# Linear attention beside a gated FFN on one core: the query projection of eight token tiles leaves the projection stage and runs as row-tiled pairs ahead of its chunk's gate/up

## The chip, the cores and the metric

The kernel runs on one core of a Trainium2 chip, in one launch, with bf16 inputs and output. The metric is the device time of one execution in microseconds (us). TensorE is called PE below, VectorE DVE, ScalarE ACT, GpSimd POOL, and SyncE, which issues nearly all DMAs, SP.

## The reference, cut to what matters

```python
# S=2048 tokens, D=576, H=32 heads of 18, F=4608
x  = A_x
xn = layernorm(x)                                   # over the 576 columns
q, k, v = split(xn @ wqkv)                          # 576 -> 3*576
phi = lambda t: where(t > 0, t + 1, exp(t)) + 1e-6
pq, pk = phi(q), phi(k)
kv  = einsum("bhsd,bhse->bhde", pk, v)              # per head 18x18
z   = sum over tokens of pk
o   = (pq @ kv) / (pq . z + 1e-6)                   # per head
return x + o @ wo + (gelu(xn @ w_gate) * (xn @ w_up)) @ w_down
```

## The kernel before, in words

The 2048 tokens are 16 tiles of 128 tokens. The kernel has two parts.

**The K stage** takes the tiles one after the other. For tile n, DVE takes the row statistics in two halves (`ln_half`, L224) and joins them (`ln_aggr`, L227), ACT makes 1/std by a Ln and an Exp (`ln_rstd`, L231 and L232), and the tile is normalised into `xn` either by DVE (`ln_norm`, L245) or by ACT (`ln_norm_act`, L240, which needs a small bias that POOL makes, L235); the string `NORM` says which. The normalised tile is transposed into `xnT`, tiles 0 and 1 by PE and a copy, the others by a DMA in the crossbar (`dma_transposes`, L273, on SP's queue). Then PE multiplies K and Q in halves of 288 columns, five matmuls to a half because 576 is four and a half times 128 (`kq_mm`, L281, and `q_first`, L289, for Q of tile 0). Each half has a PSUM bank of its own (K: 4 and 5, Q: 6 and 7), which the next tile uses again. A row of ones at row 64 of the fifth block adds 1 in the matmul, so that phi is max(min(exp(psum-1), 1), psum): ACT makes the exponential (`kq_exp`, L296) and DVE the rest (`kq_phi`, L301), into `pq` and `pk`. V is never formed: PE sums G = xn^T pk over all tiles in banks 0 to 3 (`g_accumulate`, L320, seven matmuls for a tile; a 1 in a column beside pk gives the column sums of xn), and POOL sums pk over the tiles (`z_add`, L210, called z below). `pk` lies in the store that later holds the FFN's hidden values, so its writes are named hT in the profile.

The order in which these steps are recorded is the order of each engine's queue. Each step has a time, a rank and what it must follow; `in_order` makes an order from them. In front of that stands `HEAD`, a list written out by hand, of which this kernel has about half the steps. In the list `s` is a half of the statistics, `a` the join, `r` 1/std, `b` the bias, `n` the normalisation, `c` the transpose, `m6.1.0` the matmuls of tile 6, K (1) or Q (0), half 0, `e` their exponential, `p` their phi, `z` and `G` the sums, `x` a load of two tiles of x. Across engines only semaphores order the work, not the list.

After the last tile come the rest of G (its fourth row block, L320, and a strip of 64 rows, L327), the copies of G, the small product that gives kv (L400) and the sum of z.

**The FFN part** goes over four chunks of 512 tokens. Of each chunk, 18 steps of gate and up (`gu_pair`) put two 128-column blocks each through `_Unit`, then four `_DownTile`s multiply down and add the attention's output. A `_Unit` computes two outputs in two banks. The contraction of 576 is nine blocks of 64 rows; PE is split into two row tiles of 64 that run at the same time, one on each output, and they take turns on a bank: `p1` gives the lower rows to output 0 and the upper to output 1, then an empty instruction on POOL waits for that (`relay`), and `p2` does it the other way round. Parts of neighbouring units alternate: p1 of two units, then p2 of two units. All of this is L351. The down matmuls are L750 and L755, a short row-tiled pair that opens or closes a tile is L738. Banks are handed out by a ring of eight. The denominators of the attention are made by DVE beside gate and up, one tile in four steps (`den_jobs`), 16 jobs in a chunk, tiles 0 to 3 in the first.

```python
SP queue of the FFN part: gate/up blocks (4 buffers ahead), w_down and wo in chunk 0, outputs
ACT: one table of functions holds exp and ln, another gelu; it is loaded where it changes
```

Of the kernel before, what the change touches and what calls it, by code (L numbers as in the profile page):

```python
# [8 lines left out]
ACT = mybir.ActivationFunctionType  # L9
# [31 lines left out]
XW = 640  # L41
KLO = HP + 1
Q_CUT = 3
PKW = 578


class _Ring:
# [11 lines left out]
def kernel(  # L59
# [119 lines left out]
    nc.gpsimd.memset(xn[:, :, D:XW], 0.0)  # L179
    nc.gpsimd.memset(xn[:, :, D:D + 1], 1.0)  # L180
    nc.gpsimd.memset(wqkv_sb[HP:HP + 1, 4, 0:2 * D], 1.0)
    nc.gpsimd.memset(pk[:, :, 0:1], 1.0)
    nc.gpsimd.memset(pk[:, :, D + 1:D + 2], 1.0)

    bmask = const.tile([P, CR], F32, name="bmask")
    g_sb = apool.tile([P, KT, D], BF16, name="g_sb")
# [21 lines left out]

    def z_add(n):
        nc.gpsimd.tensor_tensor(  # L210
            out=z_bf[:] if n == NS - 1 else z_sum[:], in0=pk[:, 0, 1:D + 1] if n == 1 else z_sum[:], in1=pk[:, n, 1:D + 1],
            op=ALU.add,
        )

# [84 lines left out]

    def kq_phi(n, which, hf):  # L300
        nc.vector.scalar_tensor_tensor(  # L301
            out=(pq, pk)[which][:, n, which + hf * HALF:which + (hf + 1) * HALF], in0=e_tiles[n, which, hf][:], scalar=1.0,
            in1=ps_all[:, KQ_BANK[which] + hf, :HALF], op0=ALU.min, op1=ALU.max,
        )

    G_A = {
        0: [(0, 0, 0, 288), (1, 0, 288, 289)],
        2: [(2, 0, 0, 288), (3, 0, 288, 289)],  # L310
        1: [(0, 288, 0, 224), (1, 289, 224, 223), (2, 288, 447, 130)],
    }
    G_B = {3: [(4, 0, 0, 288), (5, 0, 288, 289)]}
    STRIP = ((6, 0, 1, 0), (7, HALF + 1, 0, HALF))
    eps_sum = const.tile([P, KT], F32, name="eps_sum")

    def g_accumulate(n, pieces):
        for kt, ps_ in pieces.items():
            for b, col, d0, w in ps_:
                nc.tensor.matmul(  # L320
                    ps_all[:, b, col:col + w], lhsT=xn[:, n, kt * P:(kt + 1) * P], rhs=pk[:, n, 1 + d0:1 + d0 + w],
                    start=(n == 0 and col == 0), stop=(n == NS - 1), skip_group_check=True,
                )

    def g_strip(n):
        for rows, (b, c0, _, _) in zip((LO, HI), STRIP):
            nc.tensor.matmul(  # L327
                ps_all[rows, b, 0:HALF + 1], lhsT=xn[:, n, 4 * P:D], rhs=pk[:, n, c0:c0 + HALF + 1],
                start=(n == 0), stop=(n == NS - 1), skip_group_check=True,
            )  # L330

# [127 lines left out]
        steps[name] = _Step(*args, **kw)  # L459

    GL = 0.0
    NORM = "DDDAADADADADADAD"
    COPY = ("DVE", "ACT")
    LEAD = (-9.0, 0.5, -0.5, -0.5)
    X_AT = [3.35, 4.40, 6.30, 8.80] + [10.40] * 4
    W_AT = {1: 5.60, 0: (7.65, 8.45)}

    for n0 in range(8, NS, 2):
        step(("x", n0), "SP", 0.50, n0 - 5.5, [], lambda n0=n0: load_x(n0, 2), ready=1.6 * n0 + 2.0, tail=3.0)
    for n in range(NS):  # L470
        lead = LEAD[n] if n < 4 else 0.0
        after_x = [("x", n // 2 * 2)] if n >= 8 else []
# [5 lines left out]
        if n < TD:  # L478
            for i, (k0, k1, eng) in enumerate([(0, 3, "ACT"), (3, KT, COPY[n])]):
                b = TP_BANK[n] - i  # L480
                if NORM[n] == "A":
                    if not i:
                        step(("bias", n), "POOL", 0.20, n - 2.1 + lead, [("rstd", n)], lambda n=n: ln_bias(n))
                    step(("norm", n, i), "ACT", (0.49, 0.36)[i], n - 2.1 + lead, [("bias", n)],
                         lambda n=n, k0=k0, k1=k1: ln_norm_act(n, k0 * P, min(k1 * P, D)))
                else:
                    step(("norm", n, i), "DVE", (0.26, 0.19)[i], n - 2.1 + lead, [("rstd", n)],
                         lambda n=n, k0=k0, k1=k1: ln_norm(n, k0 * P, min(k1 * P, D)), tail=0.05)
                step(("tp", n, i), "PE", (0.32, 0.21)[i] if n == 0 else (0.18, 0.12)[i], n - 1.5 + lead, [("norm", n, i)],
                     lambda n=n, k0=k0, k1=k1, b=b: transposes(n, k0, k1, b), tail=0.08)  # L490
                step(("xnT", n, i), eng, 0.27 if i else 0.44, n - 0.88 + lead, [("tp", n, i)],
                     lambda n=n, k0=k0, k1=k1, b=b, eng=eng: tp_copy(n, k0, k1, b, acopy if eng == "ACT" else vcopy), tail=0.04)
            ready = [("xnT", n, 0), ("xnT", n, 1)]
        else:
            if NORM[n] == "P":
                step(("norm", n), "POOL", 2.35, n - 2.1 - GL, [("rstd", n)], lambda n=n: ln_norm_pool(n))
            elif NORM[n] == "A":
                step(("bias", n), "POOL", 0.15, n - 2.1, [("rstd", n)], lambda n=n: ln_bias(n))
                step(("norm", n), "ACT", 0.77, n - 2.1, [("bias", n)], lambda n=n: ln_norm_act(n), tail=0.09)
            else:  # L500
                step(("norm", n), "DVE", 0.36, n - 2.1, [("rstd", n)], lambda n=n: ln_norm(n), tail=0.07)
            step(("xnT", n), "SP", 2.10, n - 1.9, [("norm", n)], lambda n=n: dma_transposes(n), tail=2.05)
            ready = [("xnT", n)]
        for which, rank in ((1, n), (0, n + 0.6)):
            for h in range(2):
                r = rank + h / 100
                free = [("phi", n - 1, which, h)] if n else []
                if n == which == 0:
                    k0, k1 = ((0, Q_CUT), (Q_CUT, KT))[h]
                    step(("mm", 0, 0, h), "PE", 0.246 * (k1 - k0), r, ready + [("mm", 0, 0, 0)][:h],  # L510
                         lambda k0=k0, k1=k1: q_first(k0, k1), ready=W_AT[0][h], tail=0.15)
                else:
                    step(("mm", n, which, h), "PE", 0.615, r, ready + free, lambda n=n, w=which, h=h: kq_mm(n, w, h),
                         ready=W_AT[which] if which else W_AT[0][1], tail=0.15)
                step(("exp", n, which, h), "ACT", 0.46, r + 0.10, [("mm", n, which, 1 if n == which == 0 else h)],
                     lambda n=n, w=which, h=h: kq_exp(n, w, h), tail=0.03)
                step(("phi", n, which, h), "DVE", 0.37, r + 0.15, [("exp", n, which, h)],
                     lambda n=n, w=which, h=h: kq_phi(n, w, h), tail=0.08)
        if n > 0:
            idle = [("bias" if NORM[n + 4] == "A" else "norm", n + 4)] if n + 4 < NS else []  # L520
            step(("z", n), "POOL", 1.40, n + 2.0, [("phi", m, 1, h) for m in (0, n) for h in range(2)] + idle + ([("z", n - 1)] if n > 1 else []),
                 lambda n=n: z_add(n))
        step(("G", n), "PE", 0.75, n + 1.15, [("phi", n, 1, 0), ("phi", n, 1, 1)], lambda n=n: g_accumulate(n, G_A))
    step(("spin",), "PE", 0.30, -1.0, [("tp", 0, 1)], lambda: spin(5))

    step(("bmask",), "POOL", 0.95, 0.2, [("norm", 2)], make_bmask)
# [2 lines left out]
    def in_order(steps):  # L529
# [15 lines left out]
        return [name for _, _, name in sorted(begun)]  # L545

    HEAD = """
        s0.1 s0.0 a0 r0 s1.1 n0.0 t0.0 n0.1 t0.1 s1.0 a1 w c0.1 s2.0 c0.0 s2.1 m0.1.1 a2 r1 r2 m0.1.0 n1.1 e0.1.1
        t1.1 n1.0 n2 p0.1.1 m0.0.0 t1.0 B s3.0 e0.1.0 s3.1 a3 m0.0.1 c1.1 c1.0 e0.0.0 r3 m1.1.1 p0.1.0 p0.0.0 s4.1
        G0 m1.1.0 e0.0.1 s4.0 b3 c2 g n3 c3 e1.1.1 s5.0 p0.0.1 m1.0.0 e1.1.0 a4 p1.1.1 m1.0.1 s5.1 r4 p1.1.0 e1.0.0  # L550
        a5 m2.1.1 b4 e1.0.1 s6.0 m2.1.0 x8 s6.1 G1 n4 p1.0.0 e2.1.0 p1.0.1 m2.0.0 a6 e2.1.1 s7.0 p2.1.0 r5 m2.0.1
        p2.1.1 n5 z1 m3.1.0 c4 r6 s7.1 e2.0.1 e2.0.0 m3.1.1 G2 c5 p2.0.1 e3.1.0 a7 p2.0.0 p3.1.0 s8.0 b6 e3.1.1
        p3.1.1 z2 m3.0.1 s8.1 n6 a8 e3.0.1 s9.0 m3.0.0 c6 e3.0.0 G3 p3.0.1 s9.1 r7 a9 x10 n7 r8 m4.1.0 e4.1.0 x12
        m4.1.1 e4.1.1 m4.0.1 z3 r9 p3.0.0 m4.0.0 c7 p4.1.0 e4.0.1 p4.1.1 e4.0.0 n9 m5.1.0 p4.0.1 G4 b8 z4 m5.1.1 n8
        e5.1.0 c9
    """
    KIND = {
        "x": "x", "s": "stats", "a": "aggr", "r": "rstd", "b": "bias", "n": "norm", "t": "tp", "c": "xnT", "m": "mm",
# [32 lines left out]
            g_plus_eps(g_sb[rows, 4, i * HALF:(i + 1) * HALF], ps_all[rows, b, c0:c0 + HALF], eps_sum[rows, 4:5], eng)  # L591


    load_w(2)
    nc.sync.dma_start(wqkv_sb[HP:P, 4, 2 * D:], A_wqkv[512:576, 2 * D:])
    for i in range(NWBUF):
        load_gu(i, 0)
        load_gu(i, 1)
    for c0, c1 in ((0, SC), (SC, S)):
        nc.sync.dma_start(xnT[HP:P, 4, c0:c1], xnT[0:HP, 4, c0:c1])  # L600
    for n in range(NS - 2):
        g_accumulate(n, G_B)
    g_accumulate(NS - 1, G_A)
# [42 lines left out]
    def gu_pair(sc, k):  # L646
# [29 lines left out]
        for i, (b, u) in enumerate(units):  # L676
            u.p2()
            gl = fwork.tile([P, SC], F32, name="gl")
            nc.scalar.activation(out=gl[:], in_=ps_all[:, b[0], :], func=ACT.Gelu_apprx_tanh)  # L679
            nc.vector.tensor_tensor(out=hT[:, GUB * k + i, :], in0=ps_all[:, b[1], :], in1=gl[:], op=ALU.mult)  # L680
            if den_jobs and i == 1 and 0 < k < NF // GUB - 1:
                job, n = den_jobs.pop(0)
                job(n)

    def m_product(c, bank):
        rows = DH * HCH[c]
# [81 lines left out]
                nc.sync.dma_start(out_view[:, self.n, :], self.res[:])  # L768

    for sc in range(NSC):  # L770
        for k in range(NF // GUB):
            gu_pair(sc, k)
            if sc == 0 and k in m_last_steps:
                m_last_steps[k]()
        while wd_loaded[0] < NF:
            load_wd_slice()

        tiles = [_DownTile(sc * TPC + j) for j in range(TPC)]
        tiles[0].pair()
        tiles[1].pair()  # L780
# [2 lines left out]
        for j, t in enumerate(tiles):  # L783
# [4 lines left out]
            for hf in range(2):  # L788
                t.down(hf, hooks if j == hf == 0 else {})
                if closed:  # L790
                    t.add(hf)
        for t in tiles[2:]:
            if sc < NSC - 1:
                t.opened = True
# [33 lines left out]
```

## Time and profile before

| what | value |
|---|---|
| five runs | 511.88 to 512.29 us, median 511.94 |
| the profiled execution | its own time 511.9 us, span 510.2 us |
| PE busy | 505.4 us (99%), 4489 matmuls, granted clock 1.00 throughout |
| DVE, ACT, POOL busy | 212.6, 137.2, 25.9 us |
| K stage until G is left over | about 5 to 57.6 us |
| rest of G, kv, z | 57.6 to 66.2 us |
| gate/up of one chunk | 70.3, then 69.9 us each |
| down of one chunk | about 40 us |
| DMA | 61.26 MB, mean 120 GB/s |

A busy time is the union of the instructions' recorded times. A matmul's record is longer than the spacing of matmuls that follow each other (286 ns against some 122 for 288 columns), so the spacing has to be read from groups: a stretch of the chain of waits divided by its count.

### The profile page before, as it was taken

How to read it: one execution, taken by the hardware profiler on the slowest of the kernel's cores; microseconds unless marked ns; L12 is line 12 of the kernel's file. 1: busy time of each engine (PE TensorE's matmuls, PEld its weight loads, DVE VectorE, ACT ScalarE, POOL GpSimd, SP SyncE). 2: the span in 40 equal slices, each digit the busy share in tenths (PEclk: the TensorE clock that was granted, in tenths of full speed). 3: DMA queues.
4: the chain of work that ended last, by engine and by line, in shares of the span. 5: the costliest groups of instructions: out<-in, count | busy, mean ns of one | idle time of the engine just before them, and what ended most of it. 6: DMA issues, size and time to landing. Idle time of an engine off the chain costs nothing.

```text
span 510.2 us, 10676 instructions
## 1 busy us (share of the span) xinstructions
PE 505.4 (99%) x4489; PEld 304.1 (60%) x4489; DVE 212.6 (42%) x449; ACT 137.2 (27%) x267; POOL 25.9 (5%) x40
## 2 busy tenths in 40 slices
PE   8999999999999999999999999999999999999997
PEld 6888854444587744444677644444777444445774
DVE  7996455655410044565210255555100356544101
ACT  6996523322400023322100033223000232232000
POOL 3444200000000000000000000000000000000000
PEclk9999999999999999999999999999999999999999
DMA  6737339999500066755300256666100565540000
GB/s 211 153 83 188 105 90 263 289 262 290 134 13 12 1 185 168 163 153 166 81 12 13 74 164 173 160 171 154 32 12 1 149 164 160 162 129 14 13 12 24
DMA packets 119162, 61.26 MB, mean 120 GB/s; under 512 B 25730, under 2 KB 118410, under 8 KB 119114
## 3 DMA queue, kind: packets, MB, share of 16 engines
q1 hardware_dynamic: 118970, 60.43, 45.2%
q8 instruction: 35, 0.57, 0.5%
q10 hardware_dynamic: 144, 0.15, 0.1%
q14 instruction: 13, 0.11, 0.1%
HBM read 52.86 MB, written 2.36 MB: 108 GB/s over the span
## 4 chain that ended last, share of the span: by engine, by line
PE 98%; DVE 1%; ACT 0%; DMA 0%; issue 0%
PE ps_all L351 55%; PE ps_all L750 28%; PE ps_all L281 7%; PE ps_all L320 3%; PE ps_all L755 3%; DMA x_sb<-in_A_x_dram 0%; PE ps_all L738 0%; PE ps_all L327 0%; DVE stats L224 0%; PE ps_all L400 0%; PE ps_all L690 0%; ACT phi_e L296 0%; ACT xnT L270 0%; DVE mv L227 0%; DVE xn L245 0%; ACT rstd L231 0%
## 5 line engine op out<-in xcount | busy, mean ns | idle before, releaser
L351 PE MATMUL ps_all<-xnT,wg 64*128 64x512 bf16 x1152 | 272.1, 376 | 0.0
L351 PE MATMUL ps_all<-xnT,wu 64*128 64x512 bf16 x1152 | 271.6, 376 | 0.0
L679 ACT ACTIVATE gl<-ps_all 128x512 f32<-128x512 f32 x144 | 86.0, 597 | 308.9 <-PE ps_all L351 308.8
L680 DVE TENSOR_TENSOR hT<-ps_all,gl 128x512 bf16<-128x512 f32 x144 | 99.6, 692 | 130.9 <-ACT gl L679 130.5
L351 PEld LDWEIGHTS <-wu 64*128 64x128 bf16 x1152 | 108.3, 94 | 68.1
L351 PEld LDWEIGHTS <-wg 64*128 64x128 bf16 x1152 | 108.3, 94 | 67.8
L750 PE MATMUL ps_all<-wd_sb,hT 128*128 128x288 bf16 (+2 forms) x1152 | 147.1, 286 | 0.0
L750 PEld LDWEIGHTS <-hT 128*128 128x128 bf16 x1152 | 110.9, 98 | 30.9 <-issue 1.3
L764 DVE TENSOR_TENSOR res<-ps_all,x_sb 128x288 bf16<-128x288 f32 (+2 forms) x32 | 13.8, 455 | 146.3 <-PE ps_all L755 88.1
L351 PE MATMUL ps_all<-xnT,wr 64*128 64x512 bf16 x288 | 54.6, 376 | 0.0
L281 PE MATMUL ps_all<-wqkv_sb,xnT 128*128 128x288 bf16 x310 | 40.7, 286 | 0.2
L281 PEld LDWEIGHTS <-xnT 128*128 128x128 bf16 x310 | 29.5, 98 | 7.5 <-ACT xnT L270 0.7
L296 ACT ACTIVATE phi_e<-ps_all,neg 128x288 f32<-128x288 f32 x64 | 30.8, 498 | 9.1 <-PE ps_all L281 6.2
L351 PEld LDWEIGHTS <-wr 64*128 64x128 bf16 x288 | 14.0, 94 | 16.7
L755 PE MATMUL ps_all<-m_sb,pqT 128*128 128x288 bf16 (+2 forms) x128 | 20.9, 286 | 0.0
L320 PE MATMUL ps_all<-hT,xn 128*128 128x288 bf16 (+4 forms) x144 | 18.8, 274 | 0.0
L210 POOL TENSOR_TENSOR z_sum<-z_sum,hT 128x576 f32<-128x576 f32 x13 | 16.3, 1250 | 18.5 <-DVE hT L301 17.8
L301 DVE SCALAR_TENSOR_TENSOR pq<-phi_e,ps_all 128x288 bf16<-128x288 f32 x32 | 14.1, 448 | 6.1 <-ACT phi_e L296 6.0
L320 PEld LDWEIGHTS <-xn 128*128 128x128 bf16 x144 | 13.9, 98 | 3.9 <-DVE hT L301 0.3
L301 DVE SCALAR_TENSOR_TENSOR hT<-phi_e,ps_all 128x288 bf16<-128x288 f32 x32 | 14.0, 448 | 2.6 <-ACT phi_e L296 2.4
L755 PEld LDWEIGHTS <-pqT 128*128 128x128 bf16 x128 | 12.4, 98 | 3.3
L224 DVE BATCH_NORM_STATS2 stats<-x_sb 128x6 f32<-128x288 bf16 x32 | 13.4, 443 | 1.0 <-DMA x_sb<-in_A_x_dram 1.0
(70 smaller groups left out, 129.7 us busy)
## 6 DMA issues: line engine op xcount, KB each, us to landing
wg<-in_B_w_gate_dram SPq DMA_DIRECT2D x72, 256.0 KB, 2.8
wu<-in_B_w_up_dram SPq DMA_DIRECT2D x72, 256.0 KB, 3.5
wd_sb<-in_B_w_down_dram SPq DMA_DIRECT2D x12, 432.0 KB, 4.9
wr<-in_B_w_gate_dram SPq DMA_DIRECT2D x72, 32.0 KB, 2.7
wr<-in_B_w_up_dram SPq DMA_DIRECT2D x72, 32.0 KB, 3.0
out_dram<-res SPq DMA_DIRECT2D x15, 144.0 KB, 1.8
wqkv_sb<-in_A_wqkv_dram SPq DMA_DIRECT2D x2, 576.0 KB, 4.8
x_sb<-in_A_x_dram SPq DMA_DIRECT2D x4, 288.0 KB, 3.2
```

What stands on the lines that cost most here:

```text
L210: nc.gpsimd.tensor_tensor(out=z_bf[:] if n == NS - 1 else z_sum[:], in0=pk[:, 0, 1:D + 1] if n == 1 else z_sum[:], in1=pk[:, n, 1:D + 1], ...
L224: nc.vector.bn_stats(out=ln_raw[n][:, h, :], in_=x_sb[:, n, h * HALF:(h + 1) * HALF])
L281: nc.tensor.matmul(ps_all[:, KQ_BANK[which] + hf, :HALF], lhsT=xnT[:, kt, n * P:(n + 1) * P], rhs=wqkv_sb[:, kt, c:c + HALF], start=(kt == ...
L296: nc.scalar.activation(out=e[:], in_=ps_all[:, KQ_BANK[which] + hf, :HALF], func=ACT.Exp, bias=neg1[:], scale=1.0,)
L301: nc.vector.scalar_tensor_tensor(out=(pq, pk)[which][:, n, which + hf * HALF:which + (hf + 1) * HALF], in0=e_tiles[n, which, hf][:], scala ...
L320: nc.tensor.matmul(ps_all[:, b, col:col + w], lhsT=xn[:, n, kt * P:(kt + 1) * P], rhs=pk[:, n, 1 + d0:1 + d0 + w], start=(n == 0 and col = ...
L351: return nc.tensor.matmul(self.outs[i], lhsT=self.lhs(i, rows, kt), rhs=self.rhs(i, rows, kt), start=start, stop=stop, skip_group_check=True,)
L679: nc.scalar.activation(out=gl[:], in_=ps_all[:, b[0], :], func=ACT.Gelu_apprx_tanh)
L680: nc.vector.tensor_tensor(out=hT[:, GUB * k + i, :], in0=ps_all[:, b[1], :], in1=gl[:], op=ALU.mult)
L750: nc.tensor.matmul(self.acc(hf), lhsT=hT[:, f, j * P:(j + 1) * P], rhs=wd_sb[:, f, self.parts[hf]], start=(f == 0 and not paired), stop=Fa ...
L755: nc.tensor.matmul(self.acc(hf), lhsT=pqT[:, c, self.ts], rhs=m_sb[:, c, self.parts[hf]], start=False, stop=(paired and c == 3), skip_grou ...
L764: nc.vector.tensor_tensor(out=self.res[:, hs], in0=self.acc(hf), in1=x_sb[:, self.n, hs], op=ALU.add)
```

## The change

Four things change.

1. For the tiles in `LATE` (6, 7, 9, 10, 11, 13, 14, 15) the K stage makes K alone. Their Q is made by `late_q` at the start of the chunk that they belong to, ahead of its gate/up: two tiles in chunk 1, three in chunk 2, three in chunk 3. Each is a `_Unit` with halves of 288 columns; p1 and p2 of neighbouring tiles alternate. Phi is there min(exp(psum), 1) + max(psum, 0): an Exp on ACT and two DVE instructions for a half. Q's weights are loaded a second time, into `wo2`, once wo is used up; ACT's table changes to exp at the start of the down part before, and back to gelu behind `late_q`.
2. `HEAD` now lists the whole K stage, in another order, and the x loads stand elsewhere among the crossbar DMAs.
3. `NORM` is another: DVE normalises tiles 0, 1, 2, 4, 6, 8, 10, 12, 14 and ACT the others. (Before, ACT had 3, 4, 6, 8, 10, 12, 14.)
4. `pk` gets four columns on either side instead of one, so that a G piece of 289 columns becomes 292, and pieces start at multiples of four elements. The copy of xnT's last rows to the upper partitions is split, chunk 0's ahead of the weight loads.

```diff
+LATE = (6, 7, 9, 10, 11, 13, 14, 15)
+PK0 = 4
-PKW = 578
+PKW = D + 2 * PK0
...
     G_A = {
-        0: [(0, 0, 0, 288), (1, 0, 288, 289)],
-        2: [(2, 0, 0, 288), (3, 0, 288, 289)],
-        1: [(0, 288, 0, 224), (1, 289, 224, 223), (2, 288, 447, 130)],
+        0: [(0, 0, 0, 288), (1, 0, 288, 292)],
+        2: [(2, 0, 0, 288), (3, 0, 288, 292)],
+        1: [(0, 288, 0, 224), (1, 292, 224, 220), (2, 288, 444, 136)],
     }
-    G_B = {3: [(4, 0, 0, 288), (5, 0, 288, 289)]}
+    G_B = {3: [(4, 0, 0, 288), (5, 0, 288, 292)]}
...
-    NORM = "DDDAADADADADADAD"
+    NORM = "DDDADADADADADADA"
...
-        for which, rank in ((1, n), (0, n + 0.6)):
+        for which, rank in ((1, n), (0, n + 0.6))[:1 if n in LATE else 2]:
...
     HEAD = """
...
+        s0.1 s0.0 a0 s1.0 r0 n0.0 n0.1 t0.0 t0.1 s1.1 a1 c0.1 c0.0 w s2.0 m0.1.0 s2.1 r1 a2 r2 n1.0 e0.1.0 n1.1
+        m0.1.1 t1.0 n2 p0.1.0 t1.1 m0.0.0 c1.0 m0.0.1 c1.1 s3.0 s3.1 e0.1.1 p0.1.1 B m1.1.0 a3 e0.0.1 m1.1.1 p0.0.1
+        e0.0.0 s4.0 r3 p0.0.0 e1.1.0 G0 s4.1 b3 n3 m1.0.1 e1.1.1 g a4 r4 c2 e1.0.1 m1.0.0 p1.1.0 s5.1 p1.1.1 s5.0
...
+        e4.1.1 a9 p4.1.1 b7 s8.0 z3 p3.0.1 n7 m5.1.1 s8.1 e5.1.0 G4 r9 e5.1.1 p5.1.0 c6 a8 e4.0.0 s11.0 m4.0.1 r8
+        m6.1.0 e4.0.1 p5.1.1 m6.1.1 s10.1 p4.0.0 n8 b9 s11.1 e6.1.0 e6.1.1 p6.1.0 G5 n9 m5.0.0 x12 p6.1.1 e5.0.0 a11
+        p4.0.1 c7 m7.1.0 m7.1.1 z4 s10.0 s13.0 e7.1.0 e7.1.1 a10 G6 c8 x14 m5.0.1 p7.1.0 p7.1.1 r10 r11 s13.1 p5.0.0
+        n10 s12.1 z5 m8.1.1 s12.0 e5.0.1 a13 b11 m8.1.0 z6 e8.1.1 c9 e8.1.0 c10 p8.1.1 a12 n11 G7 p8.1.0 r12 p5.0.1
+        m8.0.0 s14.0 m9.1.1 m9.1.0 G8 r13 n12 e9.1.1 z7 b13 e9.1.0 p9.1.1 s14.1 c11 m8.0.1 n13 p9.1.0 m10.1.1 s15.0
...
+        p13.1.0 e12.0.1 e14.1.1 z11 p14.1.1 m14.1.0 e14.1.0 p14.1.0 G13 m15.1.1 e15.1.1 p12.0.1 z12 m15.1.0 e15.1.0
+        G14 p15.1.1 p15.1.0 G12 G15
...
+    class _LateQ:
+        def __init__(self, n):
+            two = [banks.next(), banks.next()]
+            self.n, self.acc = n, [ps_all[:, b, :HALF] for b in two]
+            self.unit = _Unit(
+                self.acc, lambda i, rows, kt: xnT[rows, kt, n * P:(n + 1) * P],
+                lambda i, rows, kt: wo2[rows, kt, i * HALF:(i + 1) * HALF], nc.gpsimd,
+            )
+        def end(self):
+            self.unit.p2()
+            for i, acc in enumerate(self.acc):
+                e = fwork.tile([P, SC], F32, name="gl")
+                nc.scalar.activation(out=e[:, :HALF], in_=acc, func=ACT.Exp)
+                nc.vector.tensor_scalar_min(out=e[:, :HALF], in0=e[:, :HALF], scalar1=1.0)
+                nc.vector.scalar_tensor_tensor(
+                    out=pq[:, self.n, i * HALF:(i + 1) * HALF], in0=acc, scalar=0.0, in1=e[:, :HALF], op0=ALU.max, op1=ALU.add,
+                )
+    def late_q(sc):
+        held = []
+        for n in [n for n in LATE if n // TPC == sc]:
+            held.append(_LateQ(n))
+            held[-1].unit.p1()
+            if len(held) == 2:
+                held.pop(0).end()
+        for q in held:
+            q.end()
+    def load_late_wq():
+        nc.sync.dma_start(wo2[:, 0:4, :], A_wqkv[0:512, 0:D].rearrange("(kt p) c -> p kt c", p=P))
+        for rows in (LO, HI):
+            nc.sync.dma_start(wo2[rows, 4, :], A_wqkv[512:576, 0:D])
...
     for sc in range(NSC):
+        if any(n // TPC == sc for n in LATE):
+            late_q(sc)
+            nc.scalar.preload_act_table_set("gelu_apprx_tanh_and_others")
         for k in range(NF // GUB):
             gu_pair(sc, k)
...
+        if any(n // TPC == sc + 1 for n in LATE):
+            nc.scalar.preload_act_table_set("natural_log_exp_and_others")
         tiles = [_DownTile(sc * TPC + j) for j in range(TPC)]
...
+            if sc == j == 0:
+                load_late_wq()
```

## The prediction

> **What bounds the kernel now.** I read the page's busy times first, then the chain of waits, then windows, and last the timelines of DVE and POOL in the K stage.
>
> ```profile
> PE 505.4 (99%) x4489; PEld 304.1 (60%) x4489; DVE 212.6 (42%) x449; ACT 137.2 (27%) x267; POOL 25.9 (5%) x40
> ```
>
> ```profile
> 8.52 0.65 ACT xnT L270 x2
> 9.17 0.05 issue
> 9.22 0.79 PE ps_all L281 x5
> 10.01 0.04 issue
> 10.04 0.92 PE ps_all L320 x7
> ...
> 53.21 2.45 PE ps_all L281 x20
> 55.66 0.75 PE ps_all L320 x7
> 56.41 1.23 PE ps_all L281 x10
> 57.64 4.27 PE ps_all L320 x35
> ...
> 136.52 0.25 PE ps_all L738 x4
> ...
> 177.42 69.93 PE ps_all L351 x648
> ```
>
> The chain is PE from 9.22 us to the end, with no gap after 10.04: whatever leaves PE's queue shortens the run, until another engine cannot keep up. Spacings follow from it: 2.45/20 = 0.1225 us for a matmul of 288 columns; 69.93/324 = 0.216 us for a row-tiled pair of 512, so 0.1214 for 288 by columns, and 0.125 at most by the L738 row (two pairs in 0.25 us).
>
> The other engines in the K stage, by windows (PE, PEld, DVE, ACT and POOL busy):
>
> ```profile
> 25.00:41.00 16.00, 16.00 (x137) 12.98 (x136) 15.75 (x41) 13.77 (x35) 7.06 (x8) 1.00 0.39 83
> 41.00:57.60 16.60, 16.60 (x143) 13.47 (x141) 9.19 (x22) 10.53 (x21) 6.95 (x6) 1.00 0.73 200
> ```
>
> DVE has run ahead until 41 us: it is busy 15.75 of 16.00 us, then half. The new stage ends some 10 us sooner and takes that slack away, so delays of DVE that were hidden now matter. Two such delays stand in the timelines of DVE and POOL:
>
> ```profile
> 16.58 0.45 DVE L301 SCALAR_TENSOR_TENSOR pq<-phi_e,ps_all 128x288 bf16<-128x288 f32 x1
> 16.95 0.20 DVE L227 BATCH_NORM_AGGREGATE mv<-stats 128x2 f32<-128x12 f32 x1
> 17.07 0.40 DVE L301 SCALAR_TENSOR_TENSOR pq<-phi_e,ps_all 128x288 bf16<-128x288 f32 x1
> ...
> 17.75 0.46 DVE L224 BATCH_NORM_STATS2 stats<-x_sb 128x6 f32<-128x288 bf16 x1
> 18.12 0.44 DVE L301 SCALAR_TENSOR_TENSOR hT<-phi_e,ps_all 128x288 bf16<-128x288 f32 x1
> ...
> 34.66 1.23 DVE L245 TENSOR_SCALAR xn<-x_sb,mv,rstd 128x576 bf16<-128x576 bf16 x1
> ...
> 38.06 1.55 DVE L245 TENSOR_SCALAR xn<-x_sb,mv,rstd 128x576 bf16<-128x576 bf16 x1
> ```
>
> ```profile
> 31.09 0.27 POOL L235 TENSOR_SCALAR nbias<-mv,rstd 128x1 f32<-128x1 f32 x1 [1.65 <-DVE hT L301]
> 31.32 1.29 POOL L210 TENSOR_TENSOR z_sum<-z_sum,hT 128x576 f32<-128x576 f32 x1
> ...
> 34.52 1.20 POOL L210 TENSOR_TENSOR z_sum<-z_sum,hT 128x576 f32<-128x576 f32 x1 [1.92 <-DVE hT L301]
> ...
> 38.16 1.29 POOL L210 TENSOR_TENSOR z_sum<-z_sum,hT 128x576 f32<-128x576 f32 x1 [2.13 <-DVE hT L301]
> ```
>
> A normalisation on DVE takes 0.38 to 0.43 us alone. Where it meets z on POOL it ends 0.17 us after z: 34.52 + 1.20 + 0.17 = 35.89, and 38.16 + 1.29 + 0.16 = 39.61, though the second had started 0.10 us before z. At 22.18 one kept its 0.43 us with a z that started at 22.37, 0.19 behind it, and that z took 1.30. DVE was far enough ahead that neither cost PE anything.
>
> **The change part by part.** The sum goes against the profiled execution's own 511.9 us (span 510.2), which stands at the median of 511.94.
>
> *Q of eight tiles.* 8 x 10 matmuls leave the K stage: 80 x 0.1225 = 9.80 us. 8 x 9 pairs come in ahead of gate/up: 72 x 0.122 = 8.78 (bounds 8.74 and 9.00). Net -1.02. They stand between row-tiled L738 and L351, so no change of PE's mode is added.
>
> *G pieces.* The row of 35 less one G of 0.75 is 3.52/28 = 0.1257 a matmul, half of them 288 and half 289 wide, so a 289 piece takes 0.129. By columns a 292 piece takes 0.1242. That is 0.005 for each of the 16 in G's fourth block and the 32 of the other blocks, -0.23; the 220 and 136 wide ones may give some back. I take -0.15 (0 to -0.25).
>
> *The start.* Three waits of PE end at 6.17, 9.22 and 10.04 us. The first hangs on x's landing and statistics, which stay. At 8.45 four matmuls last to 8.94, so PE waits 0.28 us for tile 1's copies, and 5 x 0.1225 behind 9.22, 0.21 for pk. In the new list both copies (c1.0, c1.1) stand ahead of more PE work, and G0 has two K halves before it instead of one, 0.61 more. I take -0.25 (+0.1 to -0.5).
>
> *The new order of DVE and POOL.* Two normalisations meet a z. Spacings, from the rows: DVE phi 0.37, statistics 0.37, join 0.12; ACT's Exp to a Ln 0.40, Ln to its Exp 0.32, that takes 0.20, the next Ln 0.11; ACT to POOL's bias 0.10; bias to z 0.20 to 0.23; z 1.20 to 1.29; z to z 0.06, the wait between POOL's dependent memsets (11.36 to 11.42).
>
> First, tile 8. Call S the start of e5.1.0. DVE: p5.1.0 at S+0.53, then a8, a statistic, p5.1.1, a statistic, p4.0.0 (0.37 + 0.12 + 4 x 0.37), n8 at S+2.50. ACT and POOL: r9 ends at S + 0.40 + 0.32 + 0.20 = 0.92, b9 at S+1.02, z4 at S+1.23, z5 at S + 1.23 + 1.20 + 0.06 = 2.49. They coincide within 0.01 us; z wins, as at 38.06. n8 ends at 2.49 + 1.20 + 0.17 = S+3.86 instead of S+2.93. Behind it stand one statistic and p6.1.0, which frees the bank of m7.1.0: it begins at 3.86 - 0.08 + 0.37 = 4.15, lasts 0.45, and 0.06 later PE may start, at S+4.66. PE left m5.1.0 at S-0.20; behind that m5.1.1, G4, m4.0.1, m6.1.0, m6.1.1, G5, m5.0.0 take 5 x 0.6125 + 2 x 0.74 = 4.55: ready at S+4.35. PE waits 0.31.
>
> Second, tile 10. T is the start of e7.1.1. DVE: p7.1.1 at T+0.53, a statistic, p5.0.0, n10 at T + 0.53 + 3 x 0.37 = 1.64. ACT: r10, r11 end at T + 0.40 + 0.32 + 0.11 + 0.32 + 0.20 = 1.35, b11 at 1.45, z6 at T+1.65. n10 ends at T+3.02; two statistics, a13 and p8.1.1 follow (begins 2.94 + 0.37 + 0.37 + 0.12 = 3.80, ends 4.25), and m9.1.1 may start at T+4.31. PE: from T-0.20 G6, m5.0.1, m8.1.1, m8.1.0, G7, m8.0.0 (2 x 0.74 + 4 x 0.6125 = 3.93), ready at T+3.73. PE waits 0.58.
>
> Together +0.89; I take +0.85, since pieces of pk that start at even places may shorten z (a 1.14 us z exists in the trace). Bounds: 0 if neither stretches, +1.9 if each costs PE its whole 0.93.
>
> The Trainium skill, "SBUF — State Buffer", section "SBUF: two separate sides", says that the port pair of DVE and GpSimd is an exclusive lock which the op that starts first holds for its whole instruction. The blocking agrees with 1.23 and 1.55 us; "first" does not by the recorded starts, since 38.06 lost to 38.16. By the rule on recorded starts n10 (T+1.64) would win over z6 (T+1.65), and the sum would be 0.55 lower.
>
> *What is hidden.* Late Q's Exps, tables and products: with three tiles the last p2 ends at 3.3 us, two Exps at about 4.5, the table (1.28) at 5.8, and the first gelu comes at 3.3 + 3.0 + 0.3 = 6.6. DVE's 12 instructions of at most 0.45 end by 6.8, the first product is due at 7.2. The table ahead of down delays chunk 0's first copy of m_sb from 138.01 to 138.44; its reader is at 142.1. Empty POOL instructions: p1's record ends 0.28 behind its last start, POOL notes it 0.04 later, PE needs 0.08 more, 0.40 of the 0.49 that lie between. Q's weights (nearest row 576 KB, 4.8 us) have 30 us on an idle SP queue, outputs alone behind them. In the K stage a transpose holds SP for 1.2 us and lands in 2.6; the last is issued at 39.6 now and used after 53; about 4 us of that are left. The earlier copy of xnT's rows waits for long finished matmuls, and the first gate/up weights, which landed at 48.8, are read at some 56.8. All of it 0, at most +0.3 together.
>
> Sum: -1.02 - 0.15 - 0.25 + 0.85 = -0.57: 511.9 - 0.57 = 511.3, or 511.4 against the median.
>
> **The rivals.** *DVE keeps the port* (or one of the meetings slips apart by 0.15 us): no stretch gives -1.42, 510.5; one stretch -0.8 to -1.1, about 511.0 or a little under. For: the meetings are ties, and starts are records. Against: at 38.06 the normalisation lost with a lead of 0.10.
>
> *K's banks turn too slowly*: in K-only tiles PE needs 1.225 + 0.74 = 1.97 us a tile, while a bank's turn is 0.49 + 0.29 + 0.04 + 0.50 + 0.03 + 0.45 + 0.06 = 1.86 us (five starts, record, lag, Exp, lag, phi, lag). Only 0.11 is spare, where the old 3.2 us a tile left over 1. If phi has one statistic (0.37) in front of it in the seven K-only turns of tiles 9 to 15, PE loses 7 x 0.26 = 1.8 us: -0.57 + 1.8, 513.1, slower. It decides from 0.11 us of delay per turn. For: DVE's 15.75 of 16. Against: by then its statistics are mostly done, and eight Q's with 16 phi, 5.8 us, left it.
>
> That the pairs run one after the other would give +8.8, 520; the L738 row speaks against it (0.25 for four).
>
> **How the numbers follow.** A measurement of this kernel tells about 0.2%, 1.0 us, from no change. The forecast, two stretches at 511.4, has 0.56; no or one stretch 0.28, nearly all of it faster by over 0.2%; slow turns 0.15; serial pairs 0.01. Of the forecast's own range, 511.0 to 512.0, nearly all is within 0.2%. So faster 0.27, same 0.57, slower 0.16. The range runs from 510.4, no stretch, to 512.4, with the boundary costs at their upper end and some slow turns.
>
> **What would show it.** In the profile after: L281's successor with 230 matmuls, and 2740 row-tiled ones; gate/up starting near 56.8 us; a DVE normalisation of 1.3 us near 24.6 and one near 29.8, each with a gap of PE behind it; PE dense elsewhere; chunks longer by 2.2, 3.3 and 3.3 us. It is wrong if those normalisations take 0.43 us (then near 510.5), or if PE has gaps before most K halves after 33 us.

## The result, and the profile after

The changed kernel takes 510.87 us (median of 27 runs, 510.62 to 511.43) against 512.02 for the kernel before in the same comparison (47 runs): a ratio of 0.9977, 95% interval 0.9972 to 0.9982. That is 1.15 us less. No run of the one kernel lies among those of the other (510.62 to 511.43 against 511.80 to 512.54), but the difference is just past the 0.2%, 1.0 us, that the forecast took as the least a measurement can tell. The forecast was 511.4, its range began at 510.4; what came is its "one stretch" case, "about 511.0 or a little under", which together with "no stretch" had a chance of 0.28, against 0.56 for the forecast's own case.

The profiled run took 510.94 us, its span is 509.2. Lines of the program stand two lower than before in the K stage: 283 is K's and Q's matmul (281 before), 247 the normalisation, 212 z, 322 G, 353 the units of row-tiled pairs, which now include late Q.

First the busy times of the engines from the page of the changed kernel (share of the span, number of instructions):

```profile
PE 504.3 (99%) x4553; PEld 303.3 (60%) x4553; DVE 215.7 (42%) x465; ACT 143.3 (28%) x273; POOL 26.6 (5%) x40
```

64 matmuls more (144 row-tiled in, 80 plain out) and still 1.1 us less of PE: the pairs run side by side. The chain of waits, start and length in us:

```profile
8.20 1.23 PE ps_all L291 x10
9.43 1.30 PE ps_all L283 x10
10.73 0.75 PE ps_all L322 x7
...
29.83 1.39 DVE xn L247
...
32.43 1.39 PE ps_all L283 x10
...
56.80 70.28 PE ps_all L353 x652
...
167.98 72.14 PE ps_all L353 x684
...
280.01 73.24 PE ps_all L353 x702
...
393.15 73.24 PE ps_all L353 x702
```

The two waits of PE at 9.22 and 10.04 are down to 1.30 for ten matmuls (0.08 over 10 x 0.1225), gate/up starts at 56.80, and the chunks are longer by 2.21, 3.31 and 3.31 us. One wait is new: a normalisation on DVE, 1.39 us of the chain, and behind it K's matmuls at 32.43. The matmul in front of them had started at 31.74, so PE lost 32.43 - 31.74 - 0.1225, by the unrounded starts 0.56 us. DVE and POOL around it, timelines of the changed kernel:

```profile
24.77 0.42 DVE L247 TENSOR_SCALAR xn<-x_sb,mv,rstd 128x576 bf16<-128x576 bf16 x1
...
29.75 1.47 DVE L247 TENSOR_SCALAR xn<-x_sb,mv,rstd 128x576 bf16<-128x576 bf16 x1
```

```profile
23.57 2.76 POOL L212 TENSOR_TENSOR z_sum<-z_sum,hT 128x576 f32<-128x576 f32 x2
...
29.78 2.63 POOL L212 TENSOR_TENSOR z_sum<-z_sum,hT 128x576 f32<-128x576 f32 x2
```

The row at 23.57 is z4 and z5 together. The same view from 24.9 us on has z5 alone:

```profile
24.93 1.40 POOL L212 TENSOR_TENSOR z_sum<-z_sum,hT 128x576 f32<-128x576 f32 x1
```

Tile 10's normalisation (29.75) met z6 (29.78) and waited it out, as forecast. Tile 8's (24.77) did not: z5 starts 0.16 behind it, and this time z is the one that is longer, 1.40 us. z takes 1.28 us for every tile now; before it was 1.20 and 1.29 by turns.

The windows of the new stage (PE, PEld, DVE, ACT, POOL busy):

```profile
16.00:32.40 16.40, 16.03 (x137) 12.92 (x135) 15.07 (x43) 14.26 (x35) 9.08 (x10) 1.00 0.58 124
32.40:48.00 15.60, 15.57 (x133) 12.71 (x133) 10.96 (x29) 12.33 (x29) 9.87 (x11) 1.00 0.58 135
```

DVE is nearly full to 32.4 us and has room after; behind 32.43 no wait of PE for K's banks shows, so they turned in time.

### The profile page after: what moved, and what is told of

Its sections match the earlier page's. It is cut to its first block, busy times and chain, and to the rows that moved or that the text cites. A ratio compares the mean times of both kernels' runs of the same rounds, so it can differ in the third digit from the quotient of the medians.

```text
span 509.2 us, 10828 instructions
## 1 busy us (share of the span) xinstructions
PE 504.3 (99%) x4553; PEld 303.3 (60%) x4553; DVE 215.7 (42%) x465; ACT 143.3 (28%) x273; POOL 26.6 (5%) x40
## 4 chain that ended last, share of the span: by engine, by line
PE 97%; DVE 1%; DMA 0%; ACT 0%; issue 0%
PE ps_all L353 57%; PE ps_all L800 28%; PE ps_all L283 5%; PE ps_all L805 3%; PE ps_all L322 3%; DMA x_sb<-in_A_x_dram 0%; PE ps_all L788 0%; PE ps_all L329 0%; DVE stats L226 0%; DVE xn L247 0%; PE ps_all L402 0%; PE ps_all L291 0%; PE ps_all L740 0%; PE ps_all L268 0%; ACT phi_e L298 0%
## 5 line engine op out<-in xcount | busy, mean ns | idle before, releaser
L714 ACT ACTIVATE gl<-ps_all 128x288 f32<-128x288 f32 x16 | 5.9, 410 | 119.0 <-PE ps_all L353 117.8
L283 PE MATMUL ps_all<-wqkv_sb,xnT 128*128 128x288 bf16 x230 | 30.9, 286 | 0.5 <-DVE hT L303 0.4
L283 PEld LDWEIGHTS <-xnT 128*128 128x128 bf16 x230 | 21.9, 98 | 5.9 <-issue 0.6
L298 ACT ACTIVATE phi_e<-ps_all,neg 128x288 f32<-128x288 f32 x48 | 23.1, 496 | 4.8 <-PE ps_all L283 2.0
```

The costliest lines, as they stand in the source:

```text
L283: nc.tensor.matmul(ps_all[:, KQ_BANK[which] + hf, :HALF], lhsT=xnT[:, kt, n * P:(n + 1) * P], rhs=wqkv_sb[:, kt, c:c + HALF], start=(kt == ...
L298: nc.scalar.activation(out=e[:], in_=ps_all[:, KQ_BANK[which] + hf, :HALF], func=ACT.Exp, bias=neg1[:], scale=1.0,)
```

## The experiments

Times beside each other are medians; the kernel before took 511.92 to 512.00 in these comparisons.

### Tile 10's meeting taken away: apart10

```
-  z5 m8.1.1 s12.0 e5.0.1 a13 b11 m8.1.0 z6 e8.1.1
+  z5 z6 m8.1.1 s12.0 e5.0.1 a13 b11 m8.1.0 e8.1.1
-  e9.1.1 z7 b13
+  e9.1.1 b13 z7
```

> The changed kernel with two additions to z moved on POOL: z6 to before tile 11's bias (it then runs near 26.5 us, where no normalisation is due), z7 to behind tile 13's bias. Nothing else moves. Theory (tile 10's normalisation loses the port to z6, and PE waits 0.56 us for it at 32.43): that normalisation takes 0.43 us again, the gap of 0.56 goes, and the time falls by 0.5, to about 510.35 us, if no other pair meets; the next normalisations, at 33.0 and 38.2 by the same shift, have z7 starting near 33.5 and z9 ending near 37.9. Rival (the gap is only the first of several waits of DVE that would follow one another, so PE waits elsewhere): the normalisation shrinks, the time stays at 510.87 within 0.1, and new gaps of PE of 0.4 to 0.5 us stand between 32 and 36.

510.45 us (510.31 to 510.99), ratio to the kernel before 0.9971, interval 0.996 to 0.9981. Timelines of DVE and POOL:

```profile
29.77 0.42 DVE L247 TENSOR_SCALAR xn<-x_sb,mv,rstd 128x576 bf16<-128x576 bf16 x1
```

```profile
26.69 1.28 POOL L212 TENSOR_TENSOR z_sum<-z_sum,hT 128x576 f32<-128x576 f32 x1 [0.33 <-DVE mv L229]
...
33.73 3.99 POOL L212 TENSOR_TENSOR z_sum<-z_sum,hT 128x576 f32<-128x576 f32 x3
```

With z6 at 26.69 the normalisation takes 0.42 us, and the median falls by 0.42; six of the eight runs lie between 510.31 and 510.55, which is the 0.5 of the theory. The profiled run was the slowest of the eight (510.99) and shows one way in which a run gets longer: the gap at 32.4 is gone, but a wait of 0.59 stands at 29.89. SP's queue, first in the changed kernel, then in apart10:

```profile
25.22 2.06 SPq L275 DMA_TRANSPOSE xnT<-xn  x1
27.34 0.57 SPq L96 DMA_DIRECT2D x_sb<-in_A_x_dram  x1
```

```profile
25.25 1.20 SPq L275 DMA_TRANSPOSE xnT<-xn  x1
26.50 1.40 SPq L96 DMA_DIRECT2D x_sb<-in_A_x_dram  x1
```

Tile 8's transpose, issued at 25.2, landed at 29.12 in the changed kernel, 3.9 us later, and at 29.84 in apart10, 4.6 us later, where the stage's other transposes land in 2.6 to 3.0; an issue of SP near 26 us is 0.8 longer than its like in both. PE wants that tile at 29.28. So the changed kernel passes by 0.16 us, and apart10's profiled run did not.

Something else moves on the DMA engines in that time. These are the DMA queues from 25.2 to 27.2 us (packets, MB, share of the 16 engines), in the changed kernel:

```profile
q1 hardware_dynamic: 511, 0.13, 69.3%
q14 instruction: 1, 0.01, 3.1%
q8 instruction: 1, 0.02, 2.9%
```

and in meet8, the next experiment, where the transpose is issued at 26.3 and lands in 2.6 us:

```profile
q8 instruction: 1, 0.02, 2.8%
q14 instruction: 1, 0.01, 1.2%
```

q1 carries the transpose. The other two queues are labelled "instruction", and in the changed kernel their two packets run while the transpose does (25.93 and 27.00, the transpose's own packets from 26.39 to 28.14); the one on q14 takes 1.00 us. In meet8, and in the two profiles of old_pk's kernel, they are over by 27.3 us, before the transpose's first packet at 27.45 or later, and q14's takes 0.3 to 0.6. The transpose issued near 13.6 us does likewise: it lands in 3.54 and 3.58 us in old_pk's two profiles, where a packet of q14 comes inside it, and in 2.57 in ten others, where that packet comes behind it. No run moves these packets on purpose, so they are the likely reason and not a shown one.

### Tile 8's meeting made: meet8

```
-  n8 b9 s11.1 e6.1.0
+  b9 s11.1 n8 e6.1.0
```

> The changed kernel with tile 8's normalisation one place later on DVE, behind tile 11's second statistic: it starts near 25.14 us instead of 24.77, and z5 at 24.93, in front of it. Theory (whoever starts first keeps the port; the prediction's first meeting failed only by its start): the normalisation ends 0.17 behind z5, at 26.38, takes 1.2 to 1.3 us, z5 falls from 1.40 back to 1.28, and tile 6's first phi starts at 26.30 instead of 25.48 and ends at 26.75; PE, ready for tile 7's first half at 26.69, waits 0.1 us, and more if the 0.8 us by which DVE is behind reach tile 10: the forecast's price for it was 0.31. So 511.0 to 511.3 us, the likeliest 511.2. Rival (DVE keeps the port in ties and near ties, and tile 10 has another cause): 0.43 us, 510.9.

510.94 us, a little under the 511.0 to 511.3 expected. The timeline of DVE:

```profile
25.00 1.25 DVE L247 TENSOR_SCALAR xn<-x_sb,mv,rstd 128x576 bf16<-128x576 bf16 x1
```

z5 started 0.20 ahead of it, at 24.80, and took 1.28 instead of 1.40: the port went to the other. PE waited 0.11 us at 26.66, and 0.56 again at 32.40. So a meeting of tile 8 that has the statistic in front of it costs 0.1 us, and does not reach tile 10. This is not yet the forecast's case, where the statistic stands behind.

### The layout of pk put back: old_pk and old_pk_again

```
-PK0 = 4
+PK0 = 1
-        0: [(0, 0, 0, 288), (1, 0, 288, 292)],
+        0: [(0, 0, 0, 288), (1, 0, 288, 289)],
...
```

> The changed kernel with K's features laid out as before: one column of ones on each side, tiles of 578 columns, G in pieces of 288, 289, 224, 223 and 130. Theory (z's time is set by where its operand starts): z takes 1.20 and 1.29 us by turns again, as before, where the new layout has 1.28 for every tile, and one G takes the same 0.75 us within 0.01: the forecast's -0.15 for the pieces was too much, and the stage changes by -0.05 to +0.1. Rival 1 (the pieces are worth 0.15): the stage grows by 0.15. Rival 2 (z's times come from the order, not from the layout): 1.28 throughout. Which normalisation meets which z may change where a z is 0.08 shorter: tile 8's meeting was missed by 0.16.

> The kernel of old_pk once more, now timed. In its profile both normalisations of the forecast were long, 1.54 us at 24.73 and 1.40 at 30.10, with waits of PE of 0.39 and 0.48 behind them, and its one run took 511.3 us. Theory (z's 1.28 us instead of 1.20 is what made the forecast's first meeting fail, and the pieces of G bring 0.11): 511.3 us, 0.4 above the changed kernel. Rival (the long normalisation at 24.73 was one run's accident, since it started 0.09 ahead of z): 510.95 to 511.0.

511.3 us in its one run, then 511.09 (511.02 to 511.4 in all of the eleven runs but one of 510.82), ratio 0.9984, interval 0.9975 to 0.9993. DVE and POOL of old_pk:

```profile
24.73 1.54 DVE L247 TENSOR_SCALAR xn<-x_sb,mv,rstd 128x576 bf16<-128x576 bf16 x1
...
30.10 1.40 DVE L247 TENSOR_SCALAR xn<-x_sb,mv,rstd 128x576 bf16<-128x576 bf16 x1
```

```profile
23.54 2.57 POOL L212 TENSOR_TENSOR z_sum<-z_sum,hT 128x576 f32<-128x576 f32 x2
...
30.13 2.57 POOL L212 TENSOR_TENSOR z_sum<-z_sum,hT 128x576 f32<-128x576 f32 x2
```

z4 now takes 1.20 and z5 starts at 24.82, 0.09 behind the normalisation instead of 0.16, and the normalisation loses. Both meetings happen, in both profiles, and PE waits 0.39 and 0.48 us behind them: 0.87, where the forecast had 0.31 + 0.58 = 0.89. The sum agrees better than its parts: tile 8's wait is 0.08 longer, since z5 takes 1.29 us here and not 1.20, and tile 10's 0.10 shorter, half of that because the phi behind it takes 0.40 and not 0.45. The layout's z of 1.28 us is what kept tile 8's meeting out, by less than 0.1 us, but it did not do so alone. Even here the normalisation starts 0.09 ahead of z5, where the forecast had it 0.01 behind: it starts 2.44 us after the Exp e5.1.0 and not 2.50, and z5 follows z4 after 0.08 and not 0.06. The layout's 0.08 on top makes the 0.16.

From first K matmul to the first row-tiled pair it is 50.78 and 50.88 us in the two profiles, against 50.36 and 50.43 for the changed kernel (the profile of its first run and that of after_again): 0.4 more, as expected. By the medians it is 0.2, less than the runs of one kernel differ by; both profiled runs (511.3 and 511.31) are longer than the median. The 144 matmuls of G take 16.18 us from start to start here, 16.08 in the changed kernel and 16.19 before: the pieces are worth 0.11.

### Late Q back in the stage: q_in_k and q_in_k2

```
+    def kq_bank(n, which):
+        return 4 if which == 0 and n in (7, 10, 13, 15) else KQ_BANK[which]
...
-  G14 p15.1.1 p15.1.0 G12 G15
+  p15.1.1 p15.1.0 m6.0.0 m6.0.1 e6.0.0 e6.0.1 p6.0.0 p6.0.1 m7.0.0 ... p15.0.1 G14 G12 G15
...
-            late_q(sc)
-                load_late_wq()
```

(q_in_k has a 6 where q_in_k2 has the 4, which is Q's own pair of banks, and G14 and G12 in their places ahead.)

> The changed kernel with the eight late Q's back in the projection stage, as plain matmuls of 128 rows, at its end behind tile 15's K, on two pairs of banks in turn; the three chunks have no late Q, no tables for it, no reload of Q's weights. The list ahead is the same. Theory (the row tiles are the gain, all the rest of late Q is hidden): the three chunks shrink by 2.21 + 3.31 + 3.31 = 8.83 us, the projection stage grows by 80 x 0.1225 = 9.80, so plus 0.97: 511.85 us. Rival 1 (the gain is that of the new order at the start, late Q brings nothing): 510.9. Rival 2 (late Q has hidden costs at its boundaries that the stage lengths do not show): between the two. A wait for Q's banks at the end, where a bank pair comes back after 2.45 us against a turn of 1.86, is expected nowhere; the first G of banks 4 and 5 behind it may wait up to 0.3.

515.85 us. This kernel has all eight on one pair of banks and not on two, so it says nothing of the theory; it does show the price of a bank's turn. Its chain of waits:

```profile
49.48 0.63 PE ps_all L287 x5
50.10 0.02 issue
50.13 0.51 ACT phi_e L302
50.63 0.02 issue
50.66 0.47 DVE pq L307
51.12 0.04 issue
51.17 0.79 PE ps_all L287 x5
```

From the five matmuls of a half to the bank's next use it goes PE, Exp, phi, PE, and the next such step of the chain begins at 53.02: 1.85 us a turn, where the forecast's rival had worked out 1.86 from separate rows. With 1.225 us of PE work to cover it, PE loses 0.63 each time.

> As q_in_k, with the eight Q's really on two pairs of banks in turn (tiles 7, 10, 13 and 15 on the pair that K has left, the other four on Q's own); q_in_k had put all eight on one pair, and PE waited 0.63 us six times. G of tiles 14 and 12 now stand behind the last Q. A bank pair then comes back after 2.45 us, against a turn of 1.85. Theory (the row tiles are the gain, the rest of late Q costs nothing): the chunks give back 8.82 us, the stage grows by 80 x 0.1225 = 9.80: plus 0.98, 511.85 us. Rival 1 (the gain is that of the new order): 510.9. Rival 2 (late Q has costs at its boundaries): 511.1 to 511.6.

511.96 us, ratio 0.9999 to the kernel before. The chain of waits:

```profile
45.33 11.04 PE ps_all L287 x90
56.37 5.73 PE ps_all L326 x49
...
66.43 70.28 PE ps_all L357 x652
...
177.61 69.93 PE ps_all L357 x648
```

Ninety matmuls follow without a gap, the chunks are back at 69.93, and 1.09 us are lost against the changed kernel for 0.98 expected, with another 0.19 at the end of the span that is told of below. On balance the row-tiled pairs are the whole gain of the change: with the new order, new pieces and new start, but without them, the kernel is where it was before. The rest is not nothing, it cancels: -0.33 at the start and -0.11 in G's pieces, +0.57 for tile 10's wait, which is still there at 32.24, and -0.19 at the end of the span make -0.06, and the medians differ by 0.04.

### The parts one behind the other: serial_parts

```
-            if len(held) == 2:
+            if len(held) == 1:
```

> The changed kernel with each late Q's two parts one behind the other, instead of the next tile's first part between them. Theory (the relay through POOL is hidden only by the other tile's part): a second part may start 0.40 us behind the first part's last start instead of 0.12 (0.28 to the record's end, 0.04 to POOL, 0.08 to PE): 8 x 0.28 = 2.2 us more, 513.1 us, chunks two to four longer by 0.56, 0.84 and 0.84. Rival (the parts could follow each other as the first and second part of a gate/up unit's neighbours do, the relay being quicker than its records): 510.9.

513.05 us. The chain, with POOL's empty instruction in it:

```profile
167.70 0.63 PE ps_all L353 x10
168.33 0.03 issue
168.35 0.03 POOLq L362
168.38 0.05 issue
168.43 1.30 PE ps_all L353 x18
```

A second part starts 0.40 us behind the last start of the first (168.03 to 168.43). From gate/up's start to the last addition it takes 2.31 us more than the changed kernel, 8 x 0.29. The alternation hides all of that, as forecast.

### More late Q's: late12, apart10_late9, late9_g

```
-LATE = (6, 7, 9, 10, 11, 13, 14, 15)
+LATE = tuple(range(4, 16))
```

and the matmuls, Exps and phis of the Q's of tiles 4, 5, 8 and 12 struck from the list, with nothing in their place.

> The changed kernel with twelve late Q's instead of eight: those of tiles 4, 5, 8 and 12 leave the projection stage too, and nothing takes their place in the list. Each chunk from the second on then has four. Theory of the sum (PE sets the pace): 40 x 0.1225 - 36 x 0.1227 = 4.90 - 4.42, so 0.48 less, 510.4 us, tile 10's gap apart, whose neighbours move. Rival, the slow turns of the prediction: in stretches with K alone a tile has 1.97 us on PE against 1.86 for a bank's turn, so a statistic of 0.37 in front of phi makes PE wait 0.26 for each half: for eleven tiles up to 2.9 us, so as much as 513.3. Between the two it is told by the gaps of PE ahead of K halves from 18 us on.

512.92 us, slower than the kernel before (ratio 1.0017, 1.0008 to 1.0026). From the chain of waits:

```profile
26.35 4.58 DMA xnT<-xn
...
30.98 1.40 PE ps_all L283 x10
...
35.10 0.63 PE ps_all L283 x5
...
35.75 0.51 ACT phi_e L298
...
36.28 0.47 DVE hT L303
...
36.79 0.77 PE ps_all L283 x5
```

Two things ate the 0.48 us. Tiles 8 and 9 arrive late: PE waits 0.48 and 1.23 us for their transposes, the second of which took 4.58 us from its issue. And where a Q was struck out between two K tiles the banks do not come back in time: 0.63 and 0.20 at 36.8 and 37.6, where two K tiles stand back to back, and 0.19 at 23.7, where a G stands between, which is the rival's own case. That is 2.73 of waits for the 0.56 of tile 10's; less the 0.48 of PE's work it makes 1.7 us, of the 2.05 measured. Most of the rest is in waits of under 0.1 us behind G's, 0.37 more of them than in the changed kernel. So a bank's turn, the rival's mechanism, is here, and so is one that the forecast had taken as covered.

The same with tile 12 alone, on top of apart10, first with the list as it was, then with a G between all K tiles:

```
-  c14 b15 n15 m12.1.1          ...  p12.1.0 G10 m13.1.1 ... e13.1.0 G11 z10 ... p15.1.0 G12 G15
+  c14 b15 n15 G10 m12.1.1      ...  p12.1.0 G11 m13.1.1 ... e13.1.0 G12 z10 ... p15.1.0 G15
```

> As apart10, and tile 12's Q late as well, so that the last chunk has four. By the sum 10 x 0.1225 - 9 x 0.1225 = 0.12 less: 510.3 us, the fastest of all. Rival (slow turns of K's banks: without tile 12's Q four tiles with K alone stand in a row from tile 12 on, with 0.11 us to spare in each): waits of PE of 0.1 to 0.6 us ahead of K halves behind 37 us, and 510.5 to 511.0 us.

> As apart10_late9, with G of tile 10 moved between the K of tiles 11 and 12, and G of 11 and 12 each one tile earlier, so that every K tile from 11 on has a G behind it. Theory (apart10_late9 lost its 0.83 us at 38.45 and 39.26 because two K tiles stood back to back: 1.225 us for a bank's return against a turn of 1.86): both waits go, and by the sum it is 0.12 below apart10, 510.3 us. Rival (the 0.11 us that K, G, K, G leaves over is not enough, as the forecast's rival had it): waits of 0.05 to 0.3 us ahead of K halves behind 37 us, 510.5 to 511 us.

511.24 us and 510.89, both above apart10's 510.45: the rival won the first, by more than the 511.0 that it allowed, and half of the second. The first waits 0.63 and 0.20 us at 38.45 and 39.26, where K of tiles 11 and 12 stand back to back. In the second those are gone but for 0.07, and another wait comes up, here in its chain:

```profile
46.47 0.51 ACT phi_e L298
...
47.01 0.46 DVE hT L303
...
47.51 4.39 PE ps_all L322 x35
```

G12 had covered the turn of tile 15's last bank; pulled forward, it leaves G to wait 0.43 us for that phi. 0.43 + 0.07 - 0.12 is 0.38, the 0.4 us by which it lies above apart10. In its profiled run, the longest of eleven, tile 8's transpose was late again (4.66 us, PE waited 0.65). So apart10 with eight late Q's is the fastest version found.

### The two kernels once more: before_again and after_again

> The kernel before, unchanged, for a second profile of its start and end. The stages that the traces show differ by 0.83 us between the two kernels, the medians by 1.07 to 1.15. Theory (the rest is chance in x's landing at the start, 3.13 against 3.34 us, and in the stretch behind the last addition, 2.76 against 2.39): these change from profile to profile by 0.1 to 0.4. Rival (the end is really longer before): 2.7 to 2.8 again.

> The changed kernel, unchanged, for a second profile. Expected the same waits of PE (0.07, 0.08 and 0.56 us), the same chunks, and tile 8's transpose, issued near 25.2 us, landing anywhere from 27.8 to 29.8: PE needs it at 29.3. Theory of chance: the stretch behind the last addition differs from 2.39 by 0.1 to 0.4; rival: 2.39 again.

| us | before, two profiles | changed, two profiles |
|---|---|---|
| first K matmul | 6.17, 6.05 | 6.37, 6.15 |
| end of the last addition to the end of the span | 2.76, 2.76 | 2.39, 2.40 |

The start moves by 0.12 and 0.22 us between two profiles of one kernel and is taken for chance; the end does not move. Behind the last addition SP waits for the program's DMA semaphores in a fixed order, 0.06 us each. In the kernel before the last output's is the second of them and four more follow its landing, in the changed kernel it is the fifth and one follows: 3 x 0.06, 0.19 us. The other 0.17 is in the closing handshake of the engines, where ACT's drain ends 0.49 us behind the signal it waits for in the kernel before, in both profiles, and 0.09 in the changed one. q_in_k2 has the first and not the second, and 2.58 us. The change moves the number of DMAs, which may decide whose semaphore comes last; that was not tried by itself.

## Why the prediction was right, and where not

From first K matmul to gate/up the stage takes 56.80 - 6.37 = 50.43 us instead of 66.24 - 6.17 = 60.07, and the chunks 8.83 more, -0.81 together, for which the four terms below give -0.97 - 0.11 - 0.33 + 0.56 = -0.85. With the end (-0.37) and the start by chance (+0.15) this makes -1.03, against -1.15 of the medians.

- **Q of eight tiles**, -9.80 + 8.78 = -1.02: came as -9.80 + 8.83 = -0.97; a pair takes 0.1225 us, as a plain matmul does. q_in_k2 shows that this is the gain.
- **G pieces**, -0.15: came as -0.11 (16.19 to 16.08), old_pk giving it back, but not where the sum had it. From its start to the next one a piece of 292 takes 0.127 us, as the one of 289 did, and not 0.1242 for 0.129. What got shorter stands beside them: the pieces of 288 went from 0.124 to 0.122, the one of 223, now 220, from 0.0995 to 0.097.
- **The start**, -0.25: PE's two waits of 0.28 and 0.20 became 0.07 and 0.08, -0.33.
- **The meetings**, +0.85: this step failed by its first half. Tile 10's came at 0.56 for 0.58, in part by luck: z took 1.28 us and not the 1.20 of the sum, and the phi behind it 0.39 and not 0.45; with a z of 1.20 (old_pk) the wait was 0.48. Tile 8's, +0.31, did not come. The sum had z at 1.20 us, hoping that even places would shorten it; they made it 1.28 for all tiles, z5 came 0.08 later, and DVE kept the port. Neither error was enough alone: the sum's spacings of DVE and POOL were off by another 0.1, and without it a z of 1.28 would have left a lead of 0.07 us, and 0.08 lost in old_pk_again. With the old layout both meetings cost 0.87 us for 0.89.
- **What is hidden**: late Q's Exps, tables and relay cost nothing in the chunks (serial_parts shows the 0.29 a tile that the alternation covers). The transposes were covered too in the profiled runs, but with 0.16 us at tile 8 and not with the "about 4 us" that the forecast read off the last one; apart10, late12 and late9_g show PE waiting for tile 8's and 9's.
- **The end of the span**, not in the sum: -0.37. It was taken as fixed, so a third of what was gained came from a place that the forecast did not look at.
- **The rivals**: "one stretch" is what happened; tile 10's alone would make -0.84 by the sum, and the stages give -0.81. Slow turns did not happen: every K tile of the stage has a G or a Q behind it. Where that is missing, late12 and apart10_late9 show K's banks coming back late; the rival's own case, a G between two K tiles and DVE late, shows only small waits (0.19 in late12, 0.07 in late9_g). Its turn of 1.86 us was measured as 1.85.

The Trainium skill, "SBUF — State Buffer", section "SBUF: two separate sides", gives the port to the one that starts first. The runs narrow down what "first" means on the records: the normalisation lost with leads of 0.08 and 0.09 us (old_pk_again, old_pk), as it had with 0.10 before, and won with 0.16 against z5; against a one-column bias on POOL it won with 0.11 (38.70 and 38.81). So the rule holds in every meeting here if about 0.1 us is added to the recorded start on DVE; that is read off the records, and no run shows why. The forecast took ties as lost by DVE, which stands; what it had wrong was that tile 8's would be one.

## What to carry to other kernels

A step that runs in row-tiled pairs saves by its count of matmuls alone, here a tenth of them (72 pairs for 80 matmuls), if another unit's part stands between its two parts; the saving is a microsecond, and every queue that the shortened stage leans on has to have that much to spare. When a stage gets shorter, work out the slack of each tile's hand-over (port, bank turn, transpose), the middle ones above all, not that of the last tile. Two operations on DVE and GpSimd that come within 0.1 us of each other are better moved apart by order than left to a duration that a change of layout can shift.

## What the runs showed of the hardware

- A GpSimd addition of 128 x 576 with its bf16 operand at column 1 of tiles of 578 takes 1.20 and 1.29 us by turns; with the operand at column 4 of tiles of 584 it takes 1.28 each time. Moving it to a rounder place made the average longer.
- Tile 8's transpose, issued between 24.9 and 25.3 us, landed 3.9 to 4.7 us later in eight profiles; issued at 24.4 (late12) it took 3.2, and at 26.3 (meet8, old_pk, old_pk_again) 2.6. The slow ones share the DMA engines with two packets of the queues labelled "instruction", the fast ones do not; no run tested it.
- The stretch behind the last addition is 2.39 to 2.40, 2.57 to 2.58 or 2.76 us by the kernel, and the same within 0.01 in both profiles of one.
